# Weight combinations: sums on GpSimd one place ahead of their rounding, stores on SyncE, and a pair's operands before its last activations

## The chip, the cores and the metric

One NeuronCore of a Trainium2 chip runs the kernel. The metric is the device time of one execution in microseconds, and the median of three runs stands for a kernel. Weights, inputs and results lie in the chip's memory (HBM); work goes through SBUF and, for matmul results, PSUM.

## The reference

Local attention in chunks of 64, then a feed-forward layer with a PReLU, in float32:

```
scores = (q_c @ k_c^T) / 8            per batch, head and chunk of 64
attn   = exp(scores - max) / (sum + 1e-9)
x      = (attn @ v_c) laid out as 4608 tokens x 512
h      = x @ w_in                     w_in  512 x 2048
g      = max(h, 0) + alpha * min(h, 0)
out    = g @ w_out                    w_out 2048 x 512
```

The weights come as float64 and are brought to float32 pairs by the kernel itself.

## The kernel before

**Three passes for each product.** TensorE multiplies in a rounded 32-bit format. Each operand is therefore kept as a rounded part and the rest (a cast on ScalarE, a subtraction on VectorE), and a product is three passes: high by high, low by high, high by low.

**Tokens.** The 4608 tokens are nine blocks of 512. The first three go plainly through both products (48 steps of one slice of 128 of the inner dimension; a step is `ffn_in`, 12 matmuls at L318, and, two steps behind, `ffn_out`, 12 at L343). The other six go in three pairs by Strassen's scheme in Winograd's form: seven products of half blocks for eight. A pair has a first product (L598, eight values of j, each followed by activations L308 to L310) and a second (L714, seven products of eight blocks of six matmuls). The operands of the second are rounded by `split` (L554, L555), two blocks ahead.

**Attention runs beside it.** From half-step 42 on, 14 visits stand in the matmul order of the plain steps (`visits`; a half-step is either 12 matmuls). A visit multiplies probabilities by values for the chunk pair of two visits before (L279), and makes scores for the new one (L201). Then come the row maximum (L217, scaled by L218) and eight exponentials (L221) that read the scores in `ps_a`, the copies of the values out of `ps_a` (L304, L305, L295), the normalising (L225), a transpose in blocks (L232, into one single buffer `t3`) and eight transfers into `pT` on SyncE's queue (L239). The next visit needs `ps_a` free.

**Combinations of weights.** Strassen's products need sums of weight quarters. Each of 16 pairs of slices (eight of w_in, eight of w_out) gives four new half tiles, made once, stored to HBM in `units`, and streamed back for each pair of blocks (L536, GpSimd's queue). `combine` does it on 16 of the plain steps, at one place each: two sums of 512 columns that undo the rounding (L499), four of 256 columns (L506 to L509), then for both tiles a cast (L515) into a buffer `raw` or `more`, the rest (L516), and two stores by `keep_a` (L477, GpSimd's queue). All sums and rests are VectorE's. The quarters that need no sum are stored from the weights by the same `keep_a`.

**Buffers and order.** `t1` has two buffers, `raw` two, `more` and `ob` one; `g`, `gh` and `gl` two each. A block that is done goes from the accumulators (`ps_o0` to `ps_o3`) through `more`, `ob` and `g` (L372) to HBM, and the second half of a block is added there by GpSimd's queue (L377). A scheduling layer puts each engine's instructions into one fixed order by its own estimates; `tc.high_priority` pulls instructions forward, `tc.issue_after` keeps them behind one. TensorE's order is pinned as written. At run time every engine and every queue works strictly in its order, and waits where an instruction's inputs or buffers are not ready.

Of the kernel before, what the change touches and what calls it, by code (L numbers as in the profile page):

```python
# [10 lines left out]
F32R = mybir.dt.float32r  # L11
# [16 lines left out]
def tile_local_attention_prelu_ffn(  # L28
# [462 lines left out]
    def combine(side, j, early):  # L491

        ws = wi if side == "wi" else wo
        pair = [ws[j], ws[JF + j]]
        left, right = halves
        a = []
        for w in pair:
            t = stage.tile([P, 512], F32, name="t1")
            nc.vector.tensor_tensor(t, f32(w[:, 0]), f32(w[:, 1]), op=ALU.add)  # L499
            a.append(t)  # L500
# [5 lines left out]
        nc.vector.tensor_tensor(a22, a21, a22, op=ALU.add)  # L506
        nc.vector.tensor_tensor(a21, a11, a21, op=ALU.subtract)
        nc.vector.tensor_tensor(a11, a22, a11, op=ALU.subtract)
        nc.vector.tensor_tensor(a12, a12, a11, op=ALU.subtract)  # L509
        names = ((2, 4), (3, 1)) if side == "wi" else ((2, 3), (4, 1))  # L510
        for t, name in zip(a, names):
            which = "raw" if early else ("raw", "raw", "more")[fetched[0] % 3]
            fetched[0] += 1
            w = stage.tile([P, 2, 512], F32R, name=which, bufs=2 if which == "raw" else 1)
            nc.scalar.copy(w[:, 0], t)  # L515
            nc.vector.tensor_tensor(w[:, 1], t, f32(w[:, 0]), op=ALU.subtract)  # L516
            for half, s in zip((left, right), name):
                keep_a(side, {1: 5, 2: 6, 3: 7, 4: 3}[s], j, w[:, :, half])
# [133 lines left out]
    def operand(g, at):  # L652
# [8 lines left out]
        if at % 4 == 1:  # L661
# [8 lines left out]
    def second_product(g, b, operands, conversion, end):  # L670
# [24 lines left out]
        for i in ORDERS["wo"]:  # L695
# [8 lines left out]
            for j in range(JF):  # L704
# [3 lines left out]
                if at + AHEAD < 7 * JF:  # L708
                    operands.append(operand(g, at + AHEAD))
# [42 lines left out]
    COMBINE = (20, 22, 23, 24, 26, 29, 30, 31, 33, 35, 36, 37, 39, 40, 41, 43)  # L752
    combined = [(side, j) for side in ("wi", "wo") for j in range(JF)]
    ops, conversion = {}, []
    for n, (p, b, f) in enumerate(steps):
# [28 lines left out]
        elif n in COMBINE:  # L784

            with tc.issue_after(stages["softmax"][0].ins), tc.issue_after(stages["softmax"][1].ins):
                combine(*combined.pop(0), n in (23, 24, 25, 26, 32, 33, 34))
# [5 lines left out]
        if 2 * n + 1 in late:  # L793
            visit(*late[2 * n + 1])
        if n >= len(steps) - 3:
# [8 lines left out]
    assert not combined and not conversion and not finals  # L804
# [7 lines left out]
    for pair in range(NPAIR):  # L812
# [5 lines left out]
        for j in range(JF):  # L818
# [3 lines left out]
            if j == JF - 1:  # L822
                operands = [operand(g, at) for at in range(AHEAD)]
# [43 lines left out]
```

## Time and profile before

| what | before |
|---|---|
| median of three runs | 848.83 us (847.81 to 851.46) |
| the profiled execution's own time | 848.08 us |
| its span | 846.3 us |
| TensorE busy | 808.6 us, 96% |
| VectorE, ScalarE, GpSimd busy | 79%, 64%, 25% |
| plain steps with visits and combinations | about 174 to 350 us |
| second product of the first pair | from 437.4 us |

The profile is of one execution. Busy time says how long an engine had an instruction in work; a stall shows as idle time with the engine or transfer that ended it. Matmuls overlap, so a busy TensorE is not yet one at its best pace: 48 matmuls of the second product in a row take 11.07 us, and the same pace is what an undisturbed stretch shows elsewhere. The granted clock (1.00 is full) is given by stage.

### The profile page before, as it was taken

What the parts mean: (1) busy time and instruction counts of PE and PEld (TensorE: products, weight loads), DVE (VectorE), ACT (ScalarE), POOL (GpSimd) and SP (SyncE); (2) the same over time, 40 slices, a digit from 0 to 9 for tenths busy, and PEclk for the clock granted to TensorE, in tenths of its full rate; (3) what the DMA queues carried; (4) which work ended last, traced back from release to release, by engine and by line L of the source; (5) the groups of instructions that cost most, each with busy time, mean ns of one, the idle gap of its engine ahead of it and who ended that gap; (6) DMA issues with size and microseconds to landing.
All of it is one profiled execution on the core that took longest, in us unless ns stands there. A gap on an engine that the chain in (4) does not pass through costs nothing.

```text
span 846.3 us, 15382 instructions
## 1 busy us (share of the span) xinstructions
PE 808.6 (96%) x5248; PEld 646.1 (76%) x5248; DVE 670.9 (79%) x1267; ACT 545.5 (64%) x1392; POOL 213.0 (25%) x339
## 2 busy tenths in 40 slices
PE   4699999999798999999989999999999999999998
PEld 4567888777576778777767877777887888888886
DVE  5798999978797987676778997676789966568875
ACT  6976676656666767678775564877766546556552
POOL 3006222224244331111111242111122421112232
PEclk8999999999899999999999999999999999999999
DMA  9729787558678667687774789876567995555778
GB/s 274 212 76 332 242 257 262 175 169 214 192 234 225 203 215 259 215 259 258 255 260 149 242 221 326 276 253 225 175 209 234 240 310 181 192 186 188 244 218 236
DMA packets 74942, 192.40 MB, mean 227 GB/s; under 512 B 11888, under 2 KB 19056, under 8 KB 74736
## 3 DMA queue, kind: packets, MB, share of 16 engines
q0 software_dynamic: 38240, 127.42, 47.7%
q1 hardware_dynamic: 28480, 49.44, 18.5%
q10 hardware_dynamic: 8144, 14.56, 5.5%
q8 instruction: 42, 0.69, 0.3%
q14 instruction: 36, 0.29, 0.1%
HBM read 135.27 MB, written 42.99 MB: 211 GB/s over the span
## 4 chain that ended last, share of the span: by engine, by line
PE 66%; ACT 9%; DMA 9%; DVE 8%; SPq 4%; issue 3%; ACTq 0%; DVEq 0%; POOL 0%
PE ps_o L714 15%; PE ps_o L598 12%; PE ps_h L714 12%; PE ps_o L343 9%; PE ps_h L318 9%; PE ps_h L598 6%; SPq L239 4%; DMA pT<-t 4%; ACT pr L221 3%; DVE t L232 1%; DMA wi_a<-raw 1%; DMA v_sb<-v 1%; DMA more<-w_in 1%; PE ps_a L279 1%; DVE raw L516 1%
## 5 line engine op out<-in xcount | busy, mean ns | idle before, releaser
L343 PE MATMUL ps_o<-wo,gh 128*128 128x512 f32 x384 | 115.2, 396 | 3.2 <-ACT more L372 3.2
L318 PE MATMUL ps_h<-xh,wi 128*128 128x512 f32 x384 | 106.6, 402 | 3.0 <-DVE g L310 2.3
L318 PEld LDWEIGHTS ps_h<-xh,wi 128*128 128x128 f32 x384 | 71.9, 190 | 21.0 <-DVE g L310 2.9
L343 PEld LDWEIGHTS ps_o<-wo,gh 128*128 128x128 f32 x384 | 71.6, 188 | 20.9 <-ACT more L372 3.6
L221 ACT ACTIVATE pr<-ps_a,mx 128x64 f32<-128x64 f32 x224 | 67.2, 327 | 30.2 <-DVE mx L218 22.8
L343 PE MATMUL ps_o<-wo,gl 128*128 128x512 f32 x192 | 69.8, 395 | 0.0
L598 PE MATMUL ps_o<-wi,raw 128*128 128x512 f32 x171 | 67.9, 397 | 0.0
L598 PE MATMUL ps_o<-wo,raw 128*128 128x512 f32 x171 | 67.8, 396 | 0.0
L318 PE MATMUL ps_h<-xl,wi 128*128 128x512 f32 x192 | 54.0, 400 | 0.0
L221 ACT ACTIVATION_READ_ACCUMULATOR pr<-ps_a,mx 128x1 f32 x224 | 49.3, 220 | 0.0
L554 ACT CAST gh<-wi 128x512 fp32r<-128x512 f32 x48 | 29.9, 623 | 29.4 <-PE ps_o L714 15.1
L308 ACT ACTIVATE wo<-gh 128x512 f32<-128x512 f32 x24 | 15.2, 634 | 51.5 <-DVE gh L621 51.5
L536 POOL DMA_DIRECT2D raw<-wi_a x42 | 22.4, 532 | 103.0 <-PE ps_o L598 61.6
L536 POOL DMA_DIRECT2D raw<-wo_a x42 | 22.3, 532 | 91.9 <-PE ps_o L714 48.6
L318 PEld LDWEIGHTS ps_h<-xl,wi 128*128 128x128 f32 x192 | 36.6, 191 | 8.8
L330 ACT CAST gh<-g 128x512 fp32r<-128x512 f32 x48 | 29.8, 622 | 20.4 <-DVE g L310 15.3
L343 PEld LDWEIGHTS ps_o<-wo,gl 128*128 128x128 f32 x192 | 36.1, 188 | 8.7
L598 PE MATMUL ps_o<-wi,wo 128*128 128x512 f32 x99 | 39.3, 397 | 0.0
L598 PE MATMUL ps_o<-wo,wo 128*128 128x512 f32 x99 | 39.1, 395 | 0.0
L308 ACT ACTIVATE g<-ps_h 128x512 f32<-128x512 f32 x48 | 29.5, 614 | 13.9 <-PE ps_h L318 13.6
L598 PEld LDWEIGHTS ps_o<-wo,raw 128*128 128x128 f32 x171 | 32.2, 188 | 7.7
L598 PEld LDWEIGHTS ps_o<-wi,raw 128*128 128x128 f32 x171 | 32.1, 188 | 7.6
(242 smaller groups left out, 2281.5 us busy)
## 6 DMA issues: line engine op xcount, KB each, us to landing
raw<-wi_a POOLq DMA_DIRECT2D x42, 512.0 KB, 4.8
raw<-wo_a POOLq DMA_DIRECT2D x42, 512.0 KB, 4.5
wi<-wi_a POOLq DMA_DIRECT2D x21, 512.0 KB, 4.9
wo<-wi_a POOLq DMA_DIRECT2D x21, 512.0 KB, 4.6
wi<-wo_a POOLq DMA_DIRECT2D x21, 512.0 KB, 4.1
wo<-wo_a POOLq DMA_DIRECT2D x21, 512.0 KB, 4.2
v_sb<-v SPq DMA_DIRECT2D x28, 256.0 KB, 5.1
pT<-t SPq DMA_DIRECT2D x224, 32.0 KB, 3.7
```

The lines of the kernel that those rows point to most:

```text
L221: last = nc.scalar.activation(pr[:, g], one, AF.Exp, bias=mx[:, g], scale=SCALE, accum_out=sm[:, g])
L232: nc.vector.transpose(tb.rearrange("p j h t -> p h j t"), pr)
L239: nc.sync.dma_start(out=pT[dst, i].rearrange("p h t -> p (h t)"), in_=tb[src, j].rearrange("p h t -> p (h t)"),)
L279: pe(nc.tensor.matmul(att[c][par * C:(par + 1) * C, hp * C:(hp + 1) * C], lhsT=v_sb[rows, h * C:(h + 1) * C], rhs=p[rows, :, par * NP + hp ...
L308: nc.scalar.activation(g, h, AF.Relu, scale=-1.0)
L318: pe(nc.tensor.matmul(hps, lhsT=wi[f][:, l, k * P:(k + 1) * P], rhs=xx[:, k], start=(i == 0 and k == 0), stop=(i == 2 and k == NK - 1),))
L330: nc.scalar.copy(gh, g)
L343: pe(nc.tensor.matmul(o, lhsT=a[:, ts], rhs=wo[f][:, l], start=(f == first and i == 0), stop=(f == last and i == 2),))
L536: streamed[0] = nc.gpsimd.dma_start(out=f32(t), in_=units[side][n])
L554: hi = nc.scalar.copy(t_hi, t)
L598: pe(nc.tensor.matmul(ps, lhsT=w[:, l, k * P:(k + 1) * P], rhs=xx[:, xl], start=first and at == 0, stop=at == n - 1, skip_group_check=not ...
L714: pe(nc.tensor.matmul(ps[m], lhsT=w[:, l, m * P:(m + 1) * P], rhs=xx, start=i != 6 and j == 0 and n == 0, stop=j == JF - 1 and n == 2, ski ...
```

## The change

Three things change, and a fourth follows from them.

`combine` makes only the sums, on GpSimd, and leaves them in `t1`. A new function `round_sums` does the casts, rests and stores. Both run at 17 half-steps instead of 16 steps: at each the sums made at the place before are rounded, then the next sums are made. The stores of the rounded tiles go to SyncE's queue; the other stores stay on GpSimd's.

In the second product a third operand is prepared before the last j of the first product, in `gh` and `ob`, and the operands 3 and 4 ahead of the others (with a higher priority), operand 3 in the two buffers `g`.

```diff
-    def keep_a(side, i, j, a):
+    def keep_a(side, i, j, a, queue=nc.gpsimd):
         n, u = unit(side, i, j)
-        nc.gpsimd.dma_start(out=units[side][n][:, u], in_=f32(a))
+        queue.dma_start(out=units[side][n][:, u], in_=f32(a))
...
-    def combine(side, j, early):
+    sums_made = []
+
+    def combine(side, j):
...
-            nc.vector.tensor_tensor(t, f32(w[:, 0]), f32(w[:, 1]), op=ALU.add)
+            nc.gpsimd.tensor_tensor(t, f32(w[:, 0]), f32(w[:, 1]), op=ALU.add)
...
-        nc.vector.tensor_tensor(a22, a21, a22, op=ALU.add)
-        nc.vector.tensor_tensor(a21, a11, a21, op=ALU.subtract)
-        nc.vector.tensor_tensor(a11, a22, a11, op=ALU.subtract)
-        nc.vector.tensor_tensor(a12, a12, a11, op=ALU.subtract)
+        nc.gpsimd.tensor_tensor(a22, a21, a22, op=ALU.add)
+        nc.gpsimd.tensor_tensor(a21, a11, a21, op=ALU.subtract)
+        nc.gpsimd.tensor_tensor(a11, a22, a11, op=ALU.subtract)
+        nc.gpsimd.tensor_tensor(a12, a12, a11, op=ALU.subtract)
+        sums_made.append((side, j, a))
+
+    def round_sums(early):
+        side, j, a = sums_made.pop()
...
             nc.scalar.copy(w[:, 0], t)
             nc.vector.tensor_tensor(w[:, 1], t, f32(w[:, 0]), op=ALU.subtract)
-            for half, s in zip((left, right), name):
-                keep_a(side, {1: 5, 2: 6, 3: 7, 4: 3}[s], j, w[:, :, half])
+            for half, part in zip(halves, name):
+                keep_a(side, {1: 5, 2: 6, 3: 7, 4: 3}[part], j, w[:, :, half], nc.sync)
...
-        if at % 4 == 1:
+        if at == 2:
+            hi, lo = gp.tile([P, TB], F32R, name="gh"), stage.tile([P, TB], F32R, name="ob", bufs=1)
+        elif at == 3:
+            hi, lo = (gp.tile([P, TB], F32R, name="g") for _ in range(2))
+        elif at % 4 == 1:
...
-                if at + AHEAD < 7 * JF:
-                    operands.append(operand(g, at + AHEAD))
+
+                ahead = at + AHEAD + (at < 2)
+                if at != 2 and ahead < 7 * JF:
+                    with tc.high_priority(offset=2 * HIGH) if at < 2 else nullcontext():
+                        operands.append(operand(g, ahead))
...
-    COMBINE = (20, 22, 23, 24, 26, 29, 30, 31, 33, 35, 36, 37, 39, 40, 41, 43)
+    COMBINE = (43, 46, 49, 51, 54, 56, 59, 61, 64, 66, 69, 71, 74, 76, 79, 81, 84)
+
+    def combine_at(place):
+        if place in COMBINE:
+            with tc.issue_after(stages["softmax"][0].ins), tc.issue_after(stages["softmax"][1].ins):
+                if sums_made:
+                    round_sums(47 <= place <= 55 or 61 <= place <= 68)
+                if combined:
+                    combine(*combined.pop(0))
...
-                operands = [operand(g, at) for at in range(AHEAD)]
+                operands = [operand(g, at) for at in range(AHEAD + 1)]
```

The order of instructions moves with it. In the changed file the sums are L500 and L507 to L510, the casts L520, the rests L521, and `split` is L559 and L560. A number behind a name is that of one allocation.

VectorE before, from the transpose of the fourth visit's probabilities to the next visit's maximum and on; `t_2023` and `t_2025` are the fourth combination's sums, `t_2181` and `t_2183` the fifth's:

```order
L232 STREAM_TRANSPOSE t_2304<-pr 128x8x2x32
L331 TENSOR_TENSOR gl<-g,gh 128x512
L516 TENSOR_TENSOR raw<-t_2023,raw 128x512
L516 TENSOR_TENSOR raw<-t_2025,raw 128x512
L499 TENSOR_TENSOR t_2181<-wi_759 128x512
L499 TENSOR_TENSOR t_2183<-wi_1292 128x512
L310 SCALAR_TENSOR_TENSOR g<-ps_h,g 128x512
L217 TENSOR_REDUCE mx<-ps_a 128x4 x2
L506 TENSOR_TENSOR t_2183<-t_2183 128x256
L218 TENSOR_SCALAR mx<-mx 128x8
L507 TENSOR_TENSOR t_2183<-t_2181,t_2183 128x256
```

The same place now; `t_2151` and `t_2153` are the fourth combination's sums:

```order
L232 STREAM_TRANSPOSE t_2276<-pr 128x8x2x32
L310 SCALAR_TENSOR_TENSOR g<-ps_h,g 128x512
L521 TENSOR_TENSOR raw<-t_2151,raw 128x512
L331 TENSOR_TENSOR gl<-g,gh 128x512
L521 TENSOR_TENSOR raw<-t_2153,raw 128x512
L310 SCALAR_TENSOR_TENSOR g<-ps_h,g 128x512
L217 TENSOR_REDUCE mx<-ps_a 128x4 x2
L218 TENSOR_SCALAR mx<-mx 128x8
```

The sums are gone from between the rests and the maximum, and nothing stands between the maximum and its scaling.

ScalarE before, where the second block's second part ends and its accumulators `ps_o_2336` to `ps_o_2339` are copied out:

```order
L372 COPY ob<-ps_o_2338 128x512
L221 ACTIVATE pr,sm<-ps_a,mx 128x64 x3
L330 CAST gh<-g 128x512
L221 ACTIVATE pr,sm<-ps_a,mx 128x64
L372 COPY g<-ps_o_2339 128x512
L221 ACTIVATE pr,sm<-ps_a,mx 128x64 x4
L295 COPY xh<-ps_a 128x4x64 x2
L515 CAST raw<-t_2787 128x512
L515 CAST raw<-t_2789 128x512
L372 COPY more<-ps_o_2336 128x512
L372 COPY more<-ps_o_2337 128x512
```

And now, with the accumulators `ps_o_2326` to `ps_o_2329`:

```order
L372 COPY more<-ps_o_2326 128x512
L372 COPY more<-ps_o_2327 128x512
L221 ACTIVATE pr,sm<-ps_a,mx 128x64 x2
L372 COPY ob<-ps_o_2328 128x512
L221 ACTIVATE pr,sm<-ps_a,mx 128x64 x3
L330 CAST gh<-g 128x512
L372 COPY g<-ps_o_2329 128x512
L221 ACTIVATE pr,sm<-ps_a,mx 128x64 x3
L295 COPY xh<-ps_a 128x4x64 x2
L520 CAST raw<-t_2619 128x512
```

The copies of the first two accumulators have moved from the end to the front, and the casts behind all four.

ScalarE before, at the start of the first pair's second product, from the last j's `u` on; `wi_4589`, `wi_4736` and `wi_4885` are the operands 3, 4 and 5:

```order
L619 COPY g<-ps_o_5151 128x512
L308 ACTIVATE wo_5189<-gh 128x512
L308 ACTIVATE wi_5188<-gl 128x512
L309 ACTIVATE wo_5189<-wo_5189,alpha_sb 128x512
L308 ACTIVATE wi_5188<-ps_o_5151 128x512
L308 ACTIVATE wo_5189<-gl 128x512
L309 ACTIVATE wi_5188<-wi_5188,alpha_sb 128x512
L554 CAST t_5252<-wi_4736 128x512
L309 ACTIVATE wi_5188<-wi_5188,alpha_sb 128x512
L554 CAST gh<-wi_4589 128x512
L309 ACTIVATE wo_5189<-wo_5189,alpha_sb 128x512
L554 CAST more<-wi_4885 128x512
```

And now; `wi_5032` is operand 6:

```order
L624 COPY g<-ps_o_5155 128x512
L559 CAST g<-wi_4589 128x512
L308 ACTIVATE wo_5193<-gh 128x512
L308 ACTIVATE wi_5192<-gl 128x512
L309 ACTIVATE wo_5193<-wo_5193,alpha_sb 128x512
L308 ACTIVATE wo_5193<-gl 128x512
L309 ACTIVATE wi_5192<-wi_5192,alpha_sb 128x512
L308 ACTIVATE wi_5192<-ps_o_5155 128x512
L309 ACTIVATE wo_5193<-wo_5193,alpha_sb 128x512
L559 CAST t_5246<-wi_4736 128x512
L559 CAST gh<-wi_5032 128x512
L309 ACTIVATE wi_5192<-wi_5192,alpha_sb 128x512
```

The cast of operand 3 has moved ahead of the activations, and that of operand 4 behind one more of them.

More of the change, by code (lines that the diff above doesn't have):

```diff
@@ L783, in tile_local_attention_prelu_ffn @@
             ready += 1
[L784 to L787 removed]
+        combine_at(2 * n)
         if n == len(steps) - 8:
@@ L803, in tile_local_attention_prelu_ffn @@
     conversion.pop(0)()
-    assert not combined and not conversion and not finals
+    assert not combined and not sums_made and not conversion and not finals
     for _ in range(3):
```

4 lines of the change are left out of this document (2 added, 2 removed).

## The prediction

> **What bounds the kernel now.** I read the busy shares first, then what TensorE waited for, then the stages, then the chain of waits through the worst stage, and last the rows around each stall. The first line is the page's, the others are TensorE's waits over the whole span (total us, times, longest).
>
> ```profile
> PE 808.6 (96%) x5248; PEld 646.1 (76%) x5248; DVE 670.9 (79%) x1267; ACT 545.5 (64%) x1392; POOL 213.0 (25%) x339
> ...
> PE ps_a L279 <- issue: 4.7, 1, 4.7
> PE ps_o L343 <- ACT more L372: 3.2, 1, 3.2
> ...
> PE ps_o L714 <- DVE gl L555: 2.8, 3, 2.5
> PE ps_h L318 <- DVE g L310: 2.3, 2, 1.6
> ```
>
> TensorE is busy 96% of the span, so only its holes can be won. Four waits lie in reach of the change, single events nearly all: 4.7, 3.2, 2.5 and 1.6 us. The stages show where (columns: length, then busy us and count of PE, PEld, DVE, ACT, POOL, then granted clock, DMA share, GB/s):
>
> ```profile
> 200.00:230.00 30.00, 24.64 (x211) 19.55 (x211) 21.46 (x48) 17.13 (x66) 10.48 (x14) 0.89 0.78 217
> 230.00:260.00 30.00, 26.82 (x232) 20.92 (x230) 25.57 (x55) 21.61 (x69) 13.45 (x19) 1.00 0.76 228
> 290.00:320.00 30.00, 27.89 (x293) 22.05 (x293) 25.92 (x57) 20.18 (x69) 8.68 (x12) 1.00 0.60 195
> ```
>
> Three holes, 5.4, 3.2 and 2.1 us, fall into the stretch in which the combinations are made; VectorE is at 72 to 86% there, and in the first the clock falls to 0.89. The chain and the rows of time (start, length, what) tell how each arose:
>
> ```profile
> 204.83 8.18 DMA wi_a<-raw
> 213.74 0.69 DVE raw L516
> ...
> 310.96 2.78 PE ps_o L343 x12
> ...
> 316.54 0.89 PE ps_a L279 x29
> 317.95 2.98 PE ps_o L343 x12
> ...
> 443.10 10.14 PE ps_o L714 x35
> 453.24 11.07 PE ps_h L714 x48
> ```
>
> ```profile
> 216.15 0.75 DVE L217 TENSOR_REDUCE mx<-ps_a 128x4 f32<-128x256 f32 x2
> ...
> 221.17 0.31 PE L279 MATMUL ps_a<-pT,v_sb 64*64 64x64 f32 x2 [4.73 <-issue]
> ...
> 222.10 1.02 PE L279 MATMUL ps_a<-pT,v_sb 64*64 64x64 f32 x27 [0.63 <-DVE xl L305]
> ...
> 224.01 2.07 PE L318 MATMUL ps_h<-xh,wi 128*128 128x512 f32 x4
> ...
> 228.78 0.63 PE L343 MATMUL ps_o<-wo,gh 128*128 128x512 f32 x2
> ```
>
> At 221 a rounding (L516) waited for its buffer, whose store took 8.18 us to land. VectorE works in order, so the two sums behind it came late too, and behind those the row maximum L217 of a visit; the exponentials and the copies out of ps_a followed, and the next visit's matmuls found ps_a taken: 4.73 + 0.63 us. Then the clock was low: the 12 matmuls from 224.01 lasted to 228.78, 4.77 us against 2.78 for the 12 at 310.96, 2.0 more. **This hole costs 7.4 us.**
>
> ```profile
> 255.31 1.21 ACT L515 CAST raw<-t 128x512 fp32r<-128x512 f32 x2
> ...
> 256.35 1.15 ACT L372 COPY more<-ps_o 128x512 f32<-128x512 f32 x2
> ...
> 257.06 0.73 PE L343 MATMUL ps_o<-wo,gh 128*128 128x512 f32 x2 [3.18 <-ACT more L372]
> ...
> 304.75 0.71 DVE L232 STREAM_TRANSPOSE t<-pr 128x512 f32<-128x512 f32 x1 [2.71 <-DMA pT<-t]
> ...
> 307.90 1.20 PE L318 MATMUL ps_h<-xh,wi 128*128 128x512 f32 x4 [1.60 <-DVE g L310]
> ```
>
> At 257 the block's accumulators were emptied too late, because on ScalarE the copies into "more" stand behind a visit's exponentials and two rounding casts: **3.2 us**. At 308 a transpose waited 2.71 us for the tile that the previous pT transfers were still reading, and two roundings and a sum stood between it and the L310 that TensorE needed: **1.6 us**.
>
> The fourth hole is the start of the first pair's second product. There 35 matmuls from 443.10 took 10.14 us; at the pace of the next 48 (11.07, so 0.2306 each) they take 8.07. With the 2.54 us before them: **4.6 us**. In all 7.4 + 3.2 + 1.6 + 4.6 = 16.8 us, with a clean end at 831.3 of the 848.08 of the profiled execution; that lies 0.75 below the median of the runs, 848.83, so I predict on the profiled one and count the difference as noise.
>
> **The change part by part.** *Sums off VectorE.*
>
> ```profile
> L331 DVE TENSOR_TENSOR gl<-g,gh 128x512 fp32r<-128x512 f32 x27 | 18.4, 682 | 3.7 <-ACT gh L330 3.5
> ...
> L516 DVE TENSOR_TENSOR raw<-t,raw 128x512 fp32r<-128x512 f32 x23 | 15.4, 675 | 6.1 <-ACT raw L515 6.1
> L499 DVE TENSOR_TENSOR t<-wo 128x512 f32<-128x512 f32 x16 | 10.5, 684 | 0.0
> ...
> L508 DVE TENSOR_TENSOR t<-t,t 128x256 f32<-128x256 f32 x16 | 6.8, 423 | 0.3
> ```
>
> Each of 16 combinations drops two sums of 512 columns (0.684) and four of 256 (0.423) from VectorE: 3.06 us, 49 in all. None of it is TensorE's own time; it is worth what the stalls behind it are worth. At 221 the two sums ahead of the maximum (1.37) and the half-sum between it and its scaling L218 (0.42) are gone, and this rounding now follows the last one by three half-steps (places 51 and 54) instead of two (steps 23 and 24), 2.78 us more for the store to land: 4.57 of the wait of 5.36. With 0.8 left I take the low clock as gone: 6.6 of 7.4 won. At 308 one rounding instead of two and a sum stands between the transpose and L310 in the new order: 2 x 0.67 = 1.3 of 1.6 gone, since the transpose's own wait stays. At 257 the new order puts the copies into "more" ahead of the exponentials and the casts: all 3.2 gone. What is late next there is the copy of the fourth accumulator, behind five exponentials; its bank is filled nine matmuls, 2.1 us, after the first, which hides it.
>
> *Sums on GpSimd.* No such instruction is in the trace. The nearest rows:
>
> ```profile
> L94 POOL MEMSET wi<- 64x512 f32 x4 | 2.1, 518 | 0.4 <-POOLq L858 0.3
> ...
> L765 POOL COPY table<-xl 128x1 f32<-128x1 f32 x1 | 0.6, 570 | 54.1 <-DVE xl L300 54.1
> ...
> masks.py:197 POOL MEMSET ident<- 128x128 f32 x1 | 0.2, 198 | 0.0
> ```
>
> From 128 to 512 columns a memset grows by 320 ns: 0.83 ns a column, 91 ns fixed. A sum that runs at a memset's rate costs 0.52 and 0.30: 2.2 us a combination, the low end. One that needs a pass for each operand and the output on top of the COPY's 570 ns costs 1.85 and 1.21: 8.5 us, the high end. I take two to three passes with the memset's fixed cost, 0.94 to 1.37 and 0.52 to 0.73, so 4.0 to 5.7; middle 4.8, since the COPY is one cold instruction and the memsets are ten alike. The Trainium skill (GPSIMD Engine Reference, section 3.1) gives a two-input sum of 2048 columns 1.96 times VectorE's time, by which the six sums are estimated at 6.0 us; the gaps below that lose 1.5 us would then lose 5, for 840.3 in all; no run here shows it yet.
>
> GpSimd has the time only while the chain closes. A cast (half of 1.21) and a rounding (0.67) free the buffer, then come the sums: 0.6 + 0.67 + 4.8 = 6.1 us. The places are 41 half-steps apart over 16 combinations; a half-step is 2.78 us, a visit adds 317.95 - 316.54 = 1.41, and 12 visits lie between: (41 x 2.78 + 12 x 1.41) / 16 = 8.2 us. So it closes on average with 2.1 to spare. Three of the two-step gaps hold no visit, 5.6 us: 0.5 short each, **1.5 us lost**. Queued behind a late sum are the cast on ScalarE, the rounding on VectorE, and on GpSimd the eight accumulating stores of partial blocks.
>
> *Stores on SyncE.* 64 issues leave GpSimd and join SyncE, which issues the pT transfers that a visit's values need:
>
> ```profile
> L239 SPq DMA_DIRECT2D pT<-t x224: 507/588/1925, 173.8 to 591.3; - x112
> ...
> L170 SPq DMA_DIRECT2D v_sb<-v x28: 328/526/1590, 126.2 to 581.3; - x28
> ...
> DMA to landing us min/median/max: 1.8/3.7/7.2
> ```
>
> An issue of the same 256 KB is the v row, 0.33 to 1.59, median 0.53. Per visit (13 gaps in 45 half-steps: 45 x 2.78 / 13 + 1.41 = 11.0 us) SyncE has 8 x 0.59 + 0.53 = 5.2 us and gains 64/14 x 0.53 = 2.4: 7.6 of 11.0. Ahead of a pT group stand two to six stores, mostly of roundings that ended earlier, so they fill its idle time; I charge **1.5 us** for those that don't. No store can make a gain here, beyond what GpSimd's free queue already gives.
>
> *The pair's operands.*
>
> ```profile
> 437.40 1.55 PE L714 MATMUL ps_o<-t,raw 128*128 128x512 f32 x6
> ...
> 437.65 0.63 ACT L308 ACTIVATE wo<-gh 128x512 f32<-128x512 f32 x1 [1.97 <-DVE gh L621]
> ...
> 438.79 0.71 ACT L309 ACTIVATE wo<-wo,alpha_sb 128x512 f32<-128x512 f32 x1
> ```
>
> Operand 2 is now split whole before the last j and operand 3 before the last activations; ScalarE sat 1.97 us idle there, which covers the cast of about 0.6. In the kernel before, the low half of operand 2 wanted a buffer "gl" that the last activations still read; it now lies in "ob". Blocks of six matmuls start every 6 x 0.2306 = 1.38 us from 437.40, so operand 4 is due at 442.9. The seven activations ahead of its cast (four of 0.63, three of 0.71) run from 437.65 to 442.3, the cast ends at 442.9, but VectorE makes the low half behind one L310 more (0.67 each): 443.7, when 442.9 + 0.23 is wanted, 0.6 late. Operand 5 stands behind one more activation, two casts, an L310 and another low half, and comes 0.7 late. I leave 1.3 of 4.6: **3.3 won**. The other two pairs have no such wait beyond 0.3: nothing. Extra buffers (ob, both g) are free by then, and g is wanted again only for operand 8.
>
> Sum: 6.6 + 3.2 + 1.3 + 3.3 = 14.4 won, 1.5 + 1.5 lost, 11.4 net: 848.08 - 11.4 = 836.7.
>
> **The rivals.** *GpSimd too slow (slower than before).* If the sums take longer than 8.2 - 1.27 = 6.9 us, each rounding finds them unfinished, and casts and roundings hold ScalarE and VectorE in order 16 times. At 7.8 us the 14.4 won are eaten; at the high end, 8.5, it is 16 x 1.6 = 25.6 us lost: 848.1 - 14.4 + 25.6 = 859. Sharing memory access with VectorE would do it: the two-operand groups L331 and L516 alone take 33.8 us of 180 (170 to 350), 19% or 1.5 us in 8.2, and 5.7 + 1.5 = 7.2 would lose 5 us. The Trainium skill says just that GpSimd's SBUF interfaces are shared with VectorE and contend with its instructions of two SBUF inputs (GPSIMD Engine Reference, section 8); no run here has both at work yet. For it: nothing in the trace bounds a sum below 6.9. Against it: only the one cold COPY supports the high fixed cost. Chance 0.14.
>
> *SyncE too late.* With all of a visit's stores between transpose and transfers, a loop of L232 (0.71), 8 issues (4.7), 4.6 stores (2.4) and landing (3.7) takes 11.5 us against 11.0, and a transpose already waits 2.71 at 304.75. With issues like the slow ones (up to 1.9) it is 1 us a visit, 13 over the stretch: the holes move and about 847 comes out. Chance 0.2, part of it milder, 840 to 844.
>
> *Only the pair's start is won* (the roundings' buffers, not VectorE, set the hole at 221, and a new one opens): 848.1 - 3.3 = 844.8; counted half and half with the last.
>
> **How the numbers follow.** Forecast 836.7, own range 831 to 842, chance 0.62; late SyncE or moved holes 0.2, 840 to 848; slow GpSimd 0.14, 850 to 859; 0.04 for below 831. The 8-in-10 range is 830 to 849. About 0.5% (4.2 us) can be told from no change: faster takes the forecast and a third of the moved holes, 0.69; same 0.16; slower 0.15.
>
> **What would show it.** Right: sums of 512 columns on GpSimd below 1.4 us, VectorE busy about 15 us in any 30 between 200 and 320 instead of 21 to 26, TensorE's waits at L279, L343 and L714 below 1 us each, clock 1.00 there. Wrong: ScalarE's casts (L520) waiting on GpSimd or on a store, VectorE's L232 waiting on pT more than before, TensorE short of 29 us in any 30 between 170 and 350.

## The result, and the profile after

The changed kernel takes 854.35 us (median of 13 runs, 852.18 to 857.35) where the kernel before took 848.83 on the same chips (13 runs, 846.45 to 852.58): a ratio of 1.0061, 95% interval 1.0042 to 1.0080. It is 5.5 us slower; 836.7, 12 us faster, was predicted. The profiled execution took 856.72 us, its span is 854.9.

The page's line of busy shares, then what TensorE waited for (total us, times, longest):

```profile
PE 816.4 (95%) x5248; PEld 651.1 (76%) x5248; DVE 652.2 (76%) x1171; ACT 544.0 (64%) x1392; POOL 266.7 (31%) x371
...
PE ps_a L279 <- issue: 5.4, 2, 4.1
PE ps_h L318 <- DVE g L310: 3.5, 4, 1.6
PE ps_a L279 <- ACT xl L295: 2.5, 2, 1.8
...
PE ps_o L343 <- ACT gh L330: 2.1, 2, 1.1
```

Of the four waits of before, two are gone: the 3.2 us on the copies into `more` (L372), and the start of the first pair's second product. The other two have grown (L279 from 4.7 to 5.4, L318 on L310 from 2.3 to 3.5), and new ones stand beside them. By stage (length, then busy us and count of PE, PEld, DVE, ACT, POOL, then granted clock, DMA share, GB/s):

```profile
200.00:230.00 30.00, 23.26 (x256) 18.77 (x259) 17.71 (x33) 17.48 (x57) 16.58 (x17) 0.88 0.68 177
230.00:260.00 30.00, 30.00 (x258) 23.96 (x251) 19.43 (x34) 19.54 (x70) 18.20 (x20) 0.95 0.61 188
...
290.00:320.00 30.00, 26.62 (x224) 20.98 (x223) 21.08 (x35) 18.17 (x58) 18.31 (x18) 0.94 0.56 168
...
350.00:380.00 30.00, 27.30 (x225) 20.34 (x224) 19.44 (x37) 19.07 (x59) 3.70 (x7) 0.94 0.85 279
```

TensorE has 23.26 us in the first stretch against 24.64 before, 30.00 against 26.82 in the second, 26.62 against 27.89 from 290. The fourth row is a new hole; the same stretch in the kernel before was full:

```profile
350.00:380.00 30.00, 30.00 (x250) 24.02 (x247) 21.23 (x43) 22.47 (x78) 4.76 (x9) 1.00 0.84 272
```

The holes are not the whole loss: TensorE's busy time for the same 5248 matmuls also rose, from 808.6 to 816.4 us. Part of that is the granted clock. In these four stretches of 30 us it lacks 0.12, 0.05, 0.06 and 0.06 of full, by these rows an estimated 8.7 us of TensorE's time at most; before it lacked only 0.11, in the first, 3.3 us.

At 227 the same kind of chain as at 221 before ends in a hole of 4.08 + 0.49 us, a little shorter than the 4.73 + 0.63 of before; but another of the kind, 1.33 + 0.83, has opened at 211. Rows of time of SyncE's queue, ScalarE, VectorE and TensorE, in that order (start, length, what, idle time before it and what ended it):

```profile
201.16 5.56 SPq L239 DMA_DIRECT2D pT<-t  x8
206.81 0.53 SPq L170 DMA_DIRECT2D v_sb<-v  x1
207.44 4.19 SPq L477 DMA_DIRECT2D wi_a<-raw  x4
...
217.97 0.62 ACT L520 CAST raw<-t 128x512 fp32r<-128x512 f32 x1 [6.38 <-DMA wi_a<-raw]
...
218.62 0.69 DVE L521 TENSOR_TENSOR raw<-t,raw 128x512 fp32r<-128x512 f32 x1 [5.32 <-ACT raw L520]
...
222.27 0.75 DVE L217 TENSOR_REDUCE mx<-ps_a 128x4 f32<-128x256 f32 x2
...
227.57 0.44 PE L279 MATMUL ps_a<-pT,v_sb 64*64 64x64 f32 x2 [4.08 <-issue]
```

Two roundings ended at 201.7 and 204.0, and their stores were issued only from 207.44, behind eight pT issues of 5.56 us. The first buffer came free at 217.9: 5.7 us after its rounding the issue, and some 10 us more for the landing, which had taken 8.18 at this place before. The next cast held ScalarE for 6.38 us, the rest held VectorE for 5.32, and the row maximum of the visit stood behind it.

The groups of GpSimd and VectorE (count | busy us, mean ns of one | idle before it) show the second change:

```profile
L500 POOL TENSOR_TENSOR t<-wi 128x512 f32<-128x512 f32 x16 | 22.5, 1411 | 29.5 <-DVE raw L521 26.1 <-DVE more L521 2.8 <-DMA pT<-t 0.6
...
L509 POOL TENSOR_TENSOR t<-t,t 128x256 f32<-128x256 f32 x16 | 12.9, 804 | 1.3
...
L331 DVE TENSOR_TENSOR gl<-g,gh 128x512 fp32r<-128x512 f32 x48 | 38.7, 809 | 16.2 <-ACT gh L330 15.8
L310 DVE SCALAR_TENSOR_TENSOR g<-ps_h,g 128x512 f32<-128x512 f32 x48 | 32.4, 677 | 0.6 <-ACT g L309 0.3
...
L521 DVE TENSOR_TENSOR raw<-t,raw 128x512 fp32r<-128x512 f32 x25 | 21.3, 854 | 11.0 <-ACT raw L520 11.0
```

A sum of 512 columns takes 1.41 us on average for `wi` (1.36 for `wo`). VectorE's L331 and L521, which read two operands in SBUF, went from 683 and 675 ns to 809 and 854; L310, which reads one of its two in PSUM, did not (680 before, 677 now). VectorE's busy time fell by 18.7 us, from 670.9 to 652.2, though 49 us of work were taken from it.

### The profile page after: what moved, and what is told of

The parts are those of the page before. It is cut to its first block, busy times and chain, and to the rows that moved or that the text cites. A ratio compares the mean times of both kernels' runs of the same rounds, so it can differ in the third digit from the quotient of the medians.

```text
span 854.9 us, 15392 instructions
## 1 busy us (share of the span) xinstructions
PE 816.4 (95%) x5248; PEld 651.1 (76%) x5248; DVE 652.2 (76%) x1171; ACT 544.0 (64%) x1392; POOL 266.7 (31%) x371
## 4 chain that ended last, share of the span: by engine, by line
PE 68%; DVE 11%; DMA 9%; ACT 5%; SPq 3%; issue 3%; POOL 1%; DVEq 0%; ACTq 0%
PE ps_o L603 19%; PE ps_o L726 15%; PE ps_h L726 12%; PE ps_h L603 9%; PE ps_h L318 5%; PE ps_o L343 5%; DMA wi_a<-raw 3%; SPq L239 2%; ACT pr L221 2%; DMA wi<-kT 2%; DMA raw<-w_in 1%; DVE gl L331 1%; PE ps_a L279 1%; DVE g L310 1%; DMA wo_a<-raw 1%
## 5 line engine op out<-in xcount | busy, mean ns | idle before, releaser
L343 PE MATMUL ps_o<-wo,gh 128*128 128x512 f32 x384 | 116.8, 401 | 2.1 <-ACT gh L330 2.1
L318 PE MATMUL ps_h<-xh,wi 128*128 128x512 f32 x384 | 108.8, 408 | 3.5 <-DVE g L310 3.5
L318 PEld LDWEIGHTS ps_h<-xh,wi 128*128 128x128 f32 x384 | 72.9, 193 | 22.9 <-DVE g L310 5.4
L343 PEld LDWEIGHTS ps_o<-wo,gh 128*128 128x128 f32 x384 | 72.6, 191 | 20.4 <-ACT gh L330 3.0
L343 PE MATMUL ps_o<-wo,gl 128*128 128x512 f32 x192 | 71.0, 401 | 0.6 <-DVE gl L331 0.6
L603 PE MATMUL ps_o<-wi,raw 128*128 128x512 f32 x171 | 68.0, 398 | 0.0
L603 PE MATMUL ps_o<-wo,raw 128*128 128x512 f32 x171 | 67.8, 396 | 0.0
L318 PE MATMUL ps_h<-xl,wi 128*128 128x512 f32 x192 | 54.2, 401 | 0.0
L331 DVE TENSOR_TENSOR gl<-g,gh 128x512 fp32r<-128x512 f32 x48 | 38.7, 809 | 16.2 <-ACT gh L330 15.8
L223 DVE TENSOR_SCALAR sm<-sm 128x8 f32<-128x8 f32 x36 | 8.9, 247 | 46.4 <-ACT pr L221 44.0
L343 PEld LDWEIGHTS ps_o<-wo,gl 128*128 128x128 f32 x192 | 36.5, 190 | 10.1 <-DVE gl L331 1.4
L559 ACT CAST gh<-wi 128x512 fp32r<-128x512 f32 x45 | 28.1, 624 | 25.3 <-PE ps_o L726 9.5
L318 PEld LDWEIGHTS ps_h<-xl,wi 128*128 128x128 f32 x192 | 37.0, 193 | 8.9
L603 PE MATMUL ps_o<-wi,wo 128*128 128x512 f32 x99 | 39.3, 397 | 0.0
L603 PE MATMUL ps_o<-wo,wo 128*128 128x512 f32 x99 | 39.1, 395 | 0.0
L603 PEld LDWEIGHTS ps_o<-wi,raw 128*128 128x128 f32 x171 | 32.1, 188 | 7.8 <-DMA raw<-wi_a 0.3
```

The source lines that it names most:

```text
L223: nc.vector.tensor_scalar(sm, sm, 1e-9, None, op0=ALU.add)
L318: pe(nc.tensor.matmul(hps, lhsT=wi[f][:, l, k * P:(k + 1) * P], rhs=xx[:, k], start=(i == 0 and k == 0), stop=(i == 2 and k == NK - 1),))
L331: low = nc.vector.tensor_tensor(gl, g, f32(gh), op=ALU.subtract)
L343: pe(nc.tensor.matmul(o, lhsT=a[:, ts], rhs=wo[f][:, l], start=(f == first and i == 0), stop=(f == last and i == 2),))
L559: hi = nc.scalar.copy(t_hi, t)
L603: pe(nc.tensor.matmul(ps, lhsT=w[:, l, k * P:(k + 1) * P], rhs=xx[:, xl], start=first and at == 0, stop=at == n - 1, skip_group_check=not ...
```

## The experiments

Three theories were set against each other. **A:** on SyncE's queue the stores stand behind pT transfers, so buffers come free late. **B:** the sums on GpSimd are the cost, by their length (casts wait for them) or by stretching VectorE's instructions. **C:** the new places push the last roundings into the conversion at 340 to 360.

| run | sums on | stores on | pT on | places | us | ratio to before (95%) |
|---|---|---|---|---|---|---|
| e1 | VectorE | GpSimd | SyncE | old | 844.5 | 0.9952 (0.9928 to 0.9977) |
| e2, old operands | GpSimd | SyncE | SyncE | new | 859.5 | 1.0135 (1.0104 to 1.0166) |
| e3 | VectorE | SyncE | SyncE | new | 862.2 | 1.0166 (1.0139 to 1.0194) |
| e4 | GpSimd | GpSimd | SyncE | new | 887.0 | 1.0458 (1.0428 to 1.0488) |
| e5 | GpSimd | SyncE | SyncE | old | 863.0 | 1.0157 (1.0115 to 1.0199) |
| e6 | VectorE | SyncE | SyncE | old | 853.5 | 1.0058 (1.0035 to 1.0081) |
| e7, idle sums | both | SyncE | SyncE | old | 898.2 | 1.0573 (1.0531 to 1.0616) |
| e8 | VectorE | GpSimd | SyncE | new | 842.2 | 0.9916 (0.9886 to 0.9945) |
| e9 | VectorE | SyncE | GpSimd | new | 840.3 | 0.9878 (0.9850 to 0.9907) |
| e10, idle memsets | VectorE | SyncE | SyncE | old | 855.8 | 1.0056 (1.0035 to 1.0077) |
| e11, idle copies | VectorE | SyncE | SyncE | old | 863.8 | 1.0158 (1.0128 to 1.0188) |
| e12 | GpSimd | SyncE | ScalarE | new | 898.1 | 1.0572 (1.0536 to 1.0609) |
| e13 | GpSimd | none | SyncE | new | 849.2 | 1.0010 (0.9992 to 1.0028) |
| e14 | VectorE | none | SyncE | new | 834.5 | 0.9837 (0.9796 to 0.9878) |
| e15 | VectorE | SyncE | GpSimd | old | 839.5 | 0.9888 (0.9855 to 0.9920) |
| e16, no chain | GpSimd | none | SyncE | new | 852.8 | 1.0047 (1.0025 to 1.0069) |

All but e2 have the new operands of the pair. The scheduling layer orders the engines anew for each, so neighbours differ in some rows beyond the edit; TensorE's order is pinned.

**e1, the pair's operands alone.** The kernel before with the last three hunks of the change on `operand`, `second_product` and the pair loop (`ahead`, the buffers at 2 and 3, `AHEAD + 1`), and `combine` as it was.

> The kernel before with the change of the pair's operands alone; combinations as before. All theories of the loss put it into the combinations, so all expect the start of the first pair's second product to gain what it gained in the changed kernel, 3.3 to 4.6 us: 844 to 845.5 where the kernel before takes 848.8, no wait of TensorE on L560's counterpart above 0.5 us there, and the other three holes (4.7, 3.2, 1.6) left as they were. If it comes out at 848 or more, the gain at the pair's start is only a shift and is given back later.

Measured 844.46 against 849.07: 4.6 us won, as far as the whole hole was priced. The other holes did not stay as they were, though their sum is about the same: 1.9 and 0.6 us at L279 near 221, 5.5 at L343 near 257, and 1.6 at a visit's scores.

**e2, the combinations alone.** The changed kernel with those hunks undone.

> The changed kernel with the pair's operands as before; only the combinations are changed. If the two parts add, 854.4 + 4.5 = 858 to 859.5, that is 9 to 11 above the kernel before. If the operand part is itself the cause of some of the loss, 852 to 855.

859.48, that is 10.4 lost. 10.4 - 4.6 = 5.8, and 5.5 is the whole change: the parts add, and the loss is all in the combinations.

**e3, sums on VectorE again.**

```diff
-            nc.gpsimd.tensor_tensor(t, f32(w[:, 0]), f32(w[:, 1]), op=ALU.add)
+            nc.vector.tensor_tensor(t, f32(w[:, 0]), f32(w[:, 1]), op=ALU.add)
... (and the four of 256 columns)
```

> The changed kernel with the six sums of a combination on VectorE again, still one place ahead of their rounding and with the stores on SyncE's queue. Theory B (the sums on GpSimd: 6.4 us each, late for the casts, and stretching VectorE's two-input instructions while they run) expects the loss to go: no cast waits for a sum, VectorE's L331 falls from 809 ns to below 720, and the time is 844 to 848. Theory A (stores wait on SyncE's queue behind pT transfers and the buffers come free late) expects the holes near 211 and 227 to stay: 853 to 856. Theory C (the new places: roundings one place later run into the conversion at 340 to 358) expects VectorE, with 49 us of sums back, to be no better there: 855 to 860.

862.19: slower still, and above what any of the three expected, so at this point B looked refuted and A or C open. L331 is back at 683 ns, as B said. The new loss is at the start of the pair, where the first streamed weights come late (TensorE's waits):

```profile
PE ps_o L603 <- DMA raw<-wi_a: 11.4, 2, 8.9
```

**e4, stores on GpSimd again**, the sums there too.

```diff
-                keep_a(side, {1: 5, 2: 6, 3: 7, 4: 3}[part], j, w[:, :, half], nc.sync)
+                keep_a(side, {1: 5, 2: 6, 3: 7, 4: 3}[part], j, w[:, :, half])
```

> The changed kernel with the stores of the rounded sums on GpSimd's queue again; the sums stay on GpSimd. Theory A expects the casts' waits on buffers (11.4 us of ScalarE's idle time by the trace) and the holes at 211 and 227, about 8 us, to shrink: 846 to 849. Theory B expects no gain, rather a loss, since 4 issues of 0.5 to 1 us stand behind each 6.4 us of sums: 854 to 859. Theory C expects 854, with the holes at 352 and 357 as they are.

887.02, worse than any theory gave. The combinations fall so far behind (the last rest ends at 380, not 349) that TensorE stands 26.2 us at L603 for the first streamed weights. Undoing either of the two edits alone made it slower, so they could not be judged one by one from the changed kernel.

**e5, the old places.**

```diff
-    COMBINE = (43, 46, 49, 51, 54, 56, 59, 61, 64, 66, 69, 71, 74, 76, 79, 81, 84)
+    COMBINE = (38, 40, 44, 46, 48, 52, 58, 60, 62, 66, 70, 72, 74, 78, 80, 82, 86)
...
-                    round_sums(47 <= place <= 55 or 61 <= place <= 68)
+                    round_sums(place // 2 in (23, 24, 25, 26, 32, 33, 34))
```

> The changed kernel with its roundings back at the places of the kernel before (half-steps 40 to 86), the sums still on GpSimd one place ahead, the stores still on SyncE. Theory C (in the order that the new places make, the last two roundings stand behind the 44th and 46th L310 instead of the 42nd and 43rd, in the stretch of the conversion) expects the holes at 352 and 357 to go, 4 to 5 us: 848 to 850.5, or 843 to 846 if the places are the whole loss. Theories A and B expect no gain: 852 to 857, since GpSimd's chain and the stores' landing set the roundings' pace, not the places.

862.98: against C, and above what A and B gave. The holes at 352 and 357 did go (TensorE has 30.00 from 350 to 380), but in the old order the copies into `more`, which empty the accumulators, stand on ScalarE behind casts and a visit's exponentials, and at the first block's end they wait another 4.6 us for a store out of `more`: `L343 <- L372` 18.9 us in two holes.

**e6, stores on SyncE, nothing else.** e1 with `keep_a(..., nc.sync)` for the rounded tiles.

> The kernel before with the change of the pair's operands (844.5) and with the stores of the rounded sums on SyncE's queue; sums on VectorE, old places. Theory A (stores wait on SyncE behind eight pT issues of 5 to 8 us, and a buffer comes free that much later) expects 849 to 853 and a cast's longest wait on a buffer above 5 us where it was 3.1. Theories B and C expect 843.5 to 845.5.

853.51, 9.0 above e1 and 0.5 above theory A's range. TensorE's largest wait, and the rows that lead to the first of its two holes (VectorE, SyncE's queue, ScalarE, TensorE):

```profile
PE ps_o L343 <- ACT more L372: 20.1, 2, 11.4
...
191.83 0.65 DVE L516 TENSOR_TENSOR raw<-t,raw 128x512 fp32r<-128x512 f32 x1
...
191.94 4.95 SPq L239 DMA_DIRECT2D pT<-t  x8
197.09 0.41 SPq L170 DMA_DIRECT2D v_sb<-v  x1
197.61 3.22 SPq L477 DMA_DIRECT2D wi_a<-raw  x2
...
207.22 0.62 ACT L515 CAST raw<-t 128x512 fp32r<-128x512 f32 x1 [2.39 <-DMA wi_a<-raw]
...
208.60 1.07 ACT L372 COPY more<-ps_o 128x512 f32<-128x512 f32 x2
...
209.24 1.22 PE L343 MATMUL ps_o<-wo,gh 128*128 128x512 f32 x2 [8.74 <-ACT more L372]
```

A rounding ended at 192.5; its two stores waited for eight pT issues, the second landed at 207.15, and the cast that needed the buffer held up the copies behind it. The direction is theory A's, but not all of the 9.0 is shown to be the queue's. In all, casts waited 11.1 us for stores (4.7 in e1), but no single wait was over 2.8, where theory A named one above 5. Another part goes with order: here the copies into `more` stand behind casts at both block ends, in e1 at the second alone. How the two share is not shown. Over the 32 roundings, the time from the rest's end to the start of its second store, taken from the rows of L516 or L521 and of L477 in order, is 1.40 us on average in the kernel before, 4.08 here, 3.83 in e3, 3.48 in the changed kernel. The stores' landing hardly differs: a median of 3.8 us before, 4.4 here and 4.1 in the changed kernel.

**e7, sums that nobody reads.** e6 with eight sums on GpSimd beside each combination, whose result goes to a tile of its own:

```diff
+        for w in pair:
+            for half in (left, right, left, right):
+                nc.gpsimd.tensor_tensor(idle, f32(w[:, 0, half]), f32(w[:, 1, half]), op=ALU.add)
```

> As the run with stores on SyncE, and beside each combination eight sums of 256 columns on GpSimd whose result nobody reads (8 x 0.74 = 5.9 us, 128 in all), so that GpSimd works beside VectorE as in the changed kernel and nobody waits for it. Theory B in its form of contention expects VectorE's two-input instructions to go from about 0.68 to 0.8 us and 3 to 8 us more than the run with stores on SyncE alone; if only the chain of sums matters, at most 1 us more.

898.24, 44.7 above e6: the direction of contention, at many times the size that was expected. The page, and VectorE's group:

```profile
PE 825.7 (92%) x5248; PEld 655.8 (73%) x5248; DVE 730.1 (81%) x1267; ACT 543.5 (61%) x1392; POOL 289.4 (32%) x403
...
L331 DVE TENSOR_TENSOR gl<-g,gh 128x512 fp32r<-128x512 f32 x48 | 41.6, 867 | 16.1 <-ACT gh L330 15.9
```

VectorE has the same 1267 instructions and is busy 57.2 us longer than in e6 (672.9), beside 125.7 us of sums.

**e8, the places alone.** The changed kernel with e3's and e4's edits both.

> The changed kernel with both the sums on VectorE and the stores on GpSimd's queue: what is left of the change is the places, the rounding one place behind its sums, and the pair's operands. Theory C expects a good part of the loss here: 850 to 860, with the conversion late at 340 to 360. Theories A and B, for which the queue and GpSimd's sums are the loss, expect 844 to 847.

842.19, below every range. C falls: with the sums on VectorE and the stores on GpSimd the new places lose nothing. So, against this run, e3 loses 20 us by SyncE's queue and e4 45 by the sums on GpSimd, each alone.

**e9, pT out of the stores' way.** e3 with one line changed:

```diff
-                    nc.sync.dma_start(
+                    nc.gpsimd.dma_start(
                         out=pT[dst, i].rearrange("p h t -> p (h t)"),
```

> The run with the sums on VectorE and the stores on SyncE (862.2), with the visits' pT transfers moved from SyncE's to GpSimd's queue, so that no store stands behind them. Theory A (the stores' place behind eight pT issues is the cost of SyncE's queue) expects the time from a rounding's end to its second store's issue to fall from 3.8 us on average to below 1.5, the casts' waits on buffers to fall from 11.9 to below 5 us, and 842 to 848. If it is SyncE's queue itself (its issues, its landings) that is slow, the delay and the time stay: 858 to 863.

840.25, 21.9 below e3, and below both kernels. The delay fell from 3.83 to 0.85 us, the casts' waits on buffers from 11.9 to 4.9. SyncE's queue itself is not the cost; what stood ahead in it was. This settles A for sums on VectorE at the new places.

**e10 and e11, what GpSimd does meanwhile.** e6 with 20 memsets of 256 columns, or eight copies, in place of e7's eight sums:

```diff
+        for _ in range(20):
+            nc.gpsimd.memset(idle, 0.0)
```

```diff
-                nc.gpsimd.tensor_tensor(idle, f32(w[:, 0, half]), f32(w[:, 1, half]), op=ALU.add)
+                nc.gpsimd.tensor_copy(out=idle, in_=f32(w[:, 0, half]))
```

> As the run with sums on GpSimd that nobody reads (898.2), but with 20 memsets of 256 columns in place of each combination's eight sums: GpSimd is as long at work and reads nothing. If VectorE is slowed because both engines read operands in SBUF (theory B's contention), VectorE's L331 stays at 0.68 us, its busy time at 673, and the time at 852 to 856, like the run without any (853.5). If GpSimd's being at work, or the order that the added instructions bring, were the cause, 880 to 898.

> The same with eight copies of 256 columns on GpSimd in place of the eight sums: one operand read instead of two. If only GpSimd's instructions of two operands hold VectorE up, 852 to 856 and L331 at 0.68; if any reading of SBUF does, in proportion, L331 near 0.75 to 0.85 and 865 to 895.

Memsets 855.77, copies 863.75, against 853.51 with neither and 898.24 with sums. The groups with GpSimd at work: the memsets and L331 beside them, then the first half of the copies and L331 beside them:

```profile
L504 POOL MEMSET idle<- 128x256 f32 x320 | 116.1, 363 | 16.9
L331 DVE TENSOR_TENSOR gl<-g,gh 128x512 fp32r<-128x512 f32 x48 | 32.7, 681 | 16.2 <-ACT gh L330 16.2
...
L505 POOL COPY idle<-wi 128x256 f32<-128x256 f32 x64 | 37.9, 592 | 10.0 <-ACT wi L134 7.2
...
L331 DVE TENSOR_TENSOR gl<-g,gh 128x512 fp32r<-128x512 f32 x48 | 35.4, 737 | 16.0 <-ACT gh L330 15.8
```

116 us of memsets leave L331 at 681 ns; 75 us of copies bring it to 737, just under the range that was named for any reading, and 126 us of sums to 867. Against the kernel before, each on its own chip, e10 is where e6 is (1.0056 and 1.0058). The three runs also have the copies into `more` at the same places of ScalarE's order, so neither that order nor GpSimd's being busy can be the cause: for instructions of two inputs in SBUF it is what GpSimd reads. Memsets are not quite free: VectorE's busy time rose by 8.3 us beside them (681.2 against 672.9), nearly all of it in `tensor_scalar` instructions, which have one input.

**e12, pT on ScalarE's queue**, the changed kernel otherwise (`nc.scalar` in the line of e9).

> The changed kernel (sums on GpSimd, stores on SyncE) with the visits' pT transfers moved to ScalarE's queue, so that no store stands behind them. Sums on VectorE and free stores took 840.3. Theory A as the larger part expects most of the 14 us between 854.4 and 840.3 to go: 842 to 847, the mean delay of the second stores below 1.5 us. Theory B as the larger part (VectorE stretched by 30 us, sums of 6.4 us that the casts wait for) expects 849 to 854 with the delay gone. ScalarE issues 8 transfers more a visit, at some 0.35 us each 34 us in the stretch; if that is what counts, above 854.

898.05. The delay fell to 1.04 us, but ScalarE itself now waits behind its issues, 0.60 us each (its waits from 170 to 420):

```profile
ACT gh L330 <- DMA pT<-t: 30.6, 6, 6.8
```

So ScalarE's queue is no free place either, as the expectation allowed, and the run leaves open how A and B share the changed kernel's loss.

**e13 and e14, no stores at all.** The changed kernel, and e3, without the 64 stores; the pair's loads take units that lie ready:

```diff
-            for half, part in zip(halves, name):
-                keep_a(side, {1: 5, 2: 6, 3: 7, 4: 3}[part], j, w[:, :, half], nc.sync)
...
-        streamed[0] = nc.gpsimd.dma_start(out=f32(t), in_=units[side][n])
+        streamed[0] = nc.gpsimd.dma_start(out=f32(t), in_=units[side][6 if side == "wi" else 0])
```

> The changed kernel without the stores of the rounded sums (64 of 256 KB; the pair steps then load weights that lie ready, the same bytes): sums on GpSimd, no delay from any queue. If the sums on GpSimd are a gain once the stores are out of the way (49 us off VectorE, 30 back by contention), 834 to 839 and less than the next run. If they are a loss (6.4 us of sums that casts wait for, stretched two-input instructions), 842 to 850 and more than the next run.

> The same without stores, with the sums on VectorE one place ahead. The run with free queues took 840.3; without 16.8 MB of stores 836 to 840. The difference to the run before is the worth of the sums on GpSimd alone: I expect this one to be the faster by 4 to 10 us if theory B holds, the slower by 2 to 5 if it does not.

849.21 and 834.51: with no store in play the sums on GpSimd cost 14.7 us, more than expected. The chain in e13 near 240, rows of GpSimd, ScalarE, VectorE and TensorE:

```profile
238.46 0.74 POOL L510 TENSOR_TENSOR t<-t 128x256 f32<-128x256 f32 x1
240.65 1.29 POOL L500 TENSOR_TENSOR t<-wi 128x512 f32<-128x512 f32 x1 [1.46 <-DVE raw L521]
...
239.23 0.62 ACT L520 CAST raw<-t 128x512 fp32r<-128x512 f32 x1 [2.17 <-POOL t L510]
...
241.16 1.34 DVE L521 TENSOR_TENSOR raw<-t,raw 128x512 fp32r<-128x512 f32 x1
242.42 0.16 DVE L218 TENSOR_SCALAR mx<-mx 128x8 f32<-128x8 f32 x1
...
242.61 0.31 ACT L221 ACTIVATE pr<-ps_a,mx 128x64 f32<-128x64 f32 x1 [2.23 <-DVE mx L218]
...
245.88 0.95 PE L279 MATMUL ps_a<-pT,v_sb 64*64 64x64 f32 x29 [2.27 <-ACT xh L295]
```

A cast waited 2.17 us for the last sum; the second rest then ran beside the next sum, from 241.16 to 242.50, 1.34 us for 0.68; the maximum's scaling, the exponentials and the copies out of `ps_a` followed, and TensorE stood 2.27 us.

**e15, the old places with the free queues.** e6 with e9's line.

> The kernel before with the pair's operands, the stores on SyncE and the visits' pT transfers on GpSimd; sums on VectorE at the place of their rounding, old places. Theory A: the 9 us that SyncE's queue cost there come back, 841 to 845. Against the 840.3 of the same queues with the new places, a difference above 2.5 us would be the worth of the places and of the sums one place ahead.

839.48, 14.0 below e6. More than e6's 9.0 comes back; in this run the copies into `more` also stand earlier on ScalarE. Against e9's 840.25 the new places and the sums one place ahead gain nothing that can be measured. This and e9 are the best versions found that leave nothing out: 0.9888 and 0.9878 of the kernel before.

**e16, sums that no cast waits for.** e13 with the rounding of a weight tile in place of the sum:

```diff
-        for t, name in zip(a, names):
+        ws = wi if side == "wi" else wo
+        for t, name in zip((f32(ws[j][:, 0]), f32(ws[JF + j][:, 0])), names):
```

> The run without stores and with the sums on GpSimd (849.2), except that a rounding takes a weight tile that has long been there in place of the sum: GpSimd makes the same 96 sums, but no cast waits for them. The sums on VectorE took 834.5 here. If the 14.7 us between them come from casts and roundings that wait for late sums (the chain), 833 to 838. If they come from VectorE's two-input instructions stretched beside GpSimd (contention), 845 to 850. Shares show as a time between.

852.81: nothing is won back, it is 3.6 slower. With the chain gone the sums stand closer together (GpSimd is busy 28 to 29 us of each 30 from 200 to 290, against 20 to 23 in e13) and the roundings run beside them, their rests take 1125 ns for `wi`, and TensorE waits for VectorE elsewhere:

```profile
PE ps_h L318 <- DVE g L310: 12.3, 8, 3.8
...
L522 DVE TENSOR_TENSOR raw<-wi,raw 128x512 fp32r<-128x512 f32 x14 | 15.6, 1125 | 0.0
```

So a loss of this size needs no chain; in e16 contention makes it alone. How much of e13's own 14.7 a shorter chain would save is not shown, since taking it away also moved the sums.

## Why the prediction was wrong

**The pair's start: right, mis-sized by 1.3.** 3.3 was taken, 4.6 measured (e1). The 0.6 and 0.7 us of lateness that were kept back did not appear: the product's first 48 matmuls go at the full pace (the chain of waits after: start, length, what).

```profile
451.05 11.09 PE ps_o L726 x48
```

**The hole at 257: right, and for the reason given** (the new order puts the copies into `more` first). e5 and e6 show what that order is worth, 18.9 and 20.1 us of waits when late casts and exponentials stand ahead of the copies.

**Sums off VectorE, 6.6 at 221 and 1.3 at 308: this step failed.** It counted the 3.06 us that a combination takes off VectorE as free, put the price of GpSimd's sums on VectorE at nothing, and valued the gain by the stalls behind. In the runs GpSimd's sums give most of it back: 49 us off, 18.7 us less busy. With all stores out of the way, moving the sums costs 14.7 us (e14 to e13), and neither hole was won in the changed kernel. The sharing of SBUF access was in the working, but as something that could lengthen GpSimd's sums past a threshold of 6.9 us. They took 6.3 (all 96 in the trace, 101.5 us, over 16) and stayed below it. The price stood on the other engine. An L331 that overlaps no sum takes 0.68 us; the nine slow ones of 48 take 1.35 on average. The Trainium skill states this rule (SBUF — State Buffer, "Who interferes with whom"): a VectorE instruction with two inputs in SBUF contends with a GpSimd instruction that reads SBUF, not with one that only writes. The traces agree: L331 takes 867 ns beside sums and 681 beside memsets, and L310, with one input there, 677 to 680 beside either. The prediction names only a shorter remark of another page of the Trainium skill, and prices the sharing as longer sums on GpSimd alone. At 221 a second term of the sum failed with it: the 2.78 us of extra room for the store to land went into the 5.7 us that it stood in SyncE's queue, and the low clock that was taken as gone stayed (0.88 in that stretch).

**The length of a sum: mis-sized.** 4.8 us a combination was taken. Undisturbed rows (1.29 for 512 columns, 0.74 for 256) make 2 x 1.29 + 4 x 0.74 = 5.5, and with the disturbance it is 6.3; the estimate from the Trainium skill (GPSIMD Engine Reference, section 3.1), 6.0, was nearer than the middle of the nearest rows. By e16 casts that wait for longer sums are not needed for the loss; a longer sum also lies beside VectorE longer, and that part is in the step above.

**Stores on SyncE, 1.5 us: this step failed too.** "They fill its idle time" was argued from a mean, 7.6 of 11.0 us. But pT's eight issues come in one run of 5 to 9 us, and a rounding ends when it likes: in the changed kernel the second store of 18 of the 32 roundings was issued more than 2 us after the rounding's end (3 of 32 before). It cost up to 9.0 us in the old arrangement (e1 to e6, order included), 21.9 with sums on VectorE at the new places (e9 to e3), and about 5 in the changed kernel (854.4 to e13's 849.2, which is also relieved of the stores' traffic). Why it costs less beside sums on GpSimd is not shown. The rival "SyncE too late" had the queue right and the victim wrong: it priced pT behind the stores, and the stores behind pT were late. In the trace after, VectorE's L232 waited 4.3 us for pT, 4.6 before.

**The account.** Won: 4.6 at the pair's start. Lost: 10.4 in the combinations (e2), where 11.1 won less 3.0 lost was forecast. One way to walk through the runs: from e1's 844.5 to e14's 834.5, 10 won by the new places together with leaving out the stores; 15 lost when the sums go to GpSimd (e13); 5 lost when the stores come back. How the 10 divide is not shown. Two of the three signs that the prediction named for "wrong" showed: casts waiting on GpSimd (L520 on L510) and on stores, and short stretches of TensorE between 170 and 350; the third, L232 waiting on pT more than before, did not. Those for "right" showed in part: sums of 512 columns came out at 1.41 and 1.36 us, about the 1.4 named, and VectorE was at 17.7 to 21.1 us in the stretches shown up to 320, which waiting alone also brings; but TensorE still waited 5.4 us at L279, and the clock was below 1.00.

## What to carry to other kernels

Here work moved from VectorE to GpSimd was not off VectorE, since both read SBUF: price such a move by how long VectorE's two-input instructions run beside it, and try it first with sums that nobody reads (e7), with memsets as the control (e10). A queue's mean load does not say whether a store waits in it; look at what is issued in one run ahead of it, and put transfers that come in runs on another queue than those that a buffer waits for (here, swapping the two queues was worth 5 us beyond the operands, e1 to e15). Change the engine, the queue and the place one at a time: here, counted from e8, sums on GpSimd cost 45 us alone (e4), stores on SyncE 20 (e3), and both together 12.

## What the hardware showed beyond what was expected

The stretch falls on VectorE even in tiny instructions. In the changed kernel the row maximum's scaling (L218, eight columns) went from 172 ns on average to 327. One of them ends with the sum that it ran beside (GpSimd, then VectorE):

```profile
282.12 0.74 POOL L508 TENSOR_TENSOR t<-t 128x256 f32<-128x256 f32 x1
...
282.15 0.74 DVE L218 TENSOR_SCALAR mx<-mx 128x8 f32<-128x8 f32 x1
```

The larger ones show the same. All 15 of L331 and L521 in the changed kernel that last over 0.9 us run beside a sum from their start on (within 0.05 us), and all end 0.55 to 0.56 us after that sum's end, a little less than the 0.68 that a whole one takes. So VectorE's instruction waits for the whole of the sum, as a lock would make it, and does not share. The memsets touched L218 a little (204 ns) and L331 not at all. The sums are stretched in turn: 1.29 us alone, 1.41 and 1.36 on average for `wi` and `wo`, 1.49 and 1.41 in e16.

An issue of a pT transfer of 32 KB took 0.50 us on GpSimd (e9), 0.59 on SyncE and 0.60 on ScalarE (medians), and one of a 256 KB store 0.73 on GpSimd against 0.46 on SyncE: the small transfers were cheaper to issue on the one, the large ones on the other.
